# Two layers of segmented attention and feed-forward on one core: other costs in the planner that writes the instruction order, and another table of due times

## The chip, the cores and the metric

The kernel runs on one core of a Trainium2 chip. The metric is the device time of one launch in microseconds. Before the change three runs gave 569.62, 570.12 and 570.35 us, a median of 570.12. Profiled times below come from one more execution, which took 570.93 us; its profile spans 569.2 us from the first to the last instruction.

The engines have short names in the profile: PE multiplies matrices (PEld is its weight load), DVE is the vector engine, ACT the one for activations, POOL is GpSimd, and SP does nothing here but issue transfers.

## The reference

Input `x` has 2048 tokens of 640 numbers. Two rounds of an attention block and a feed-forward block are computed, all with the same weights, each with a residual:

```python
x = x + _A_ref(_layernorm(x, axis=-1), A_wq, A_wk, A_wv, A_wo, A_beta)
x = x + _B_ref(_layernorm(x, axis=-1), B_w1, B_w2)
x = x + _A_ref(_layernorm(x, axis=-1), A_wq, A_wk, A_wv, A_wo, A_beta)
x = x + _B_ref(_layernorm(x, axis=-1), B_w1, B_w2)
```

`_A_ref` has 32 heads of 20 numbers and cuts the tokens into four segments of 512. For each segment it does causal softmax attention inside the segment, and mixes it, by a gate per head, with a read from a memory of the earlier segments:

```python
for s in range(N):
    p = _softmax(logits, axis=-1)
    a_dot = jnp.einsum('bhqk,bhkd->bhqd', p, vs)
    pq = phi(qs)
    num = jnp.einsum('bhld,bhde->bhle', pq, M)
    den = jnp.einsum('bhld,bhd->bhl', pq, z)[..., None] + 1e-06
    o = g * (num / den) + (1.0 - g) * a_dot
    pk = phi(ks)
    M = M + jnp.einsum('bhld,bhle->bhde', pk, vs)
    z = z + jnp.einsum('bhld->bhd', pk)
```

`phi(t)` is t+1 above zero and exp(t) below. `_B_ref` is `relu(x @ w1) @ w2` with 1728 hidden units.

## The kernel before

**Stages.** Eight attention stages follow one another, layer a = 0, 1 by segment s = 0 to 3, and so do eight feed-forward stages. A stage is made of small generators, each of which yields one instruction after another:

- `lnorm` makes the normalised tokens: statistics on DVE (L858 to L860), the inverse deviation on POOL (L865, L867), the scaling on DVE (L871, tile `xn_tok`), and then the transpose to `xnT`, by a crossbar transfer on SP (L847) or by PE (L835). It serves `ln1` ahead of attention and `ln2` ahead of the feed-forward.
- `proj_kq` (L941) and `proj_v` (L988) are the projections. `relay_dma` moves a part of keys and queries through DRAM (writes L1023, reads L1036) because a head has 20 rows, and four heads share 128 partitions.
- `scores` (L1280 on PE, L1291 and L1294 for the exponential on ACT, the causal mask L1270 on POOL), `apply` (L1362: probabilities times values), `turn` (crossbar L1461, division and addition L1396 to L1414 on DVE).
- `mem_write` and `mem_read` are the memory: crossbar L1117 and L1125, `phi` on ACT and DVE (L1133, L1134, L1136; L1193 to L1200), products L1143 and L1230, and L1160 to L1219 on DVE.
- `o_turn` transposes a tile of 128 tokens of the attention's output by crossbar (L1516, tile `oT`, two buffers), `out_proj` multiplies it (L1526), and `add_half` adds the residual on DVE (L1468).
- `ffn` is L1580 (512 columns) with the ReLU on DVE (L1561) or ACT (L1562), the rest of the hidden units (L1592), and L1610 (320 columns).

PE has a mode: scores use it in four groups of rows, `apply` in four groups of columns, L1592 in halves, and all else in full.

**The order.** No loop fixes which instruction comes next. While the program is built, `Sched` in the host's Python plays all generators against a clock of its own, engine by engine, and writes down for each engine the order that comes out, with semaphore waits where an operand comes from elsewhere. On the chip each engine runs its list strictly in order. The rule is:

- `_best` works out for each waiting instruction when it could start: when its operands are ready, its buffers free, and its engine free. An instruction with several engines to choose from (`evac`: DVE or ACT) gets the one that ends it first.
- `run` takes the instruction with the earliest start; among equals the one with the earlier due time. Due times come from `TABLE`, a packed list with one number for each instruction, which `ranked` unpacks. So there are two passes: a first one that only finds the instructions' names, and a second one with the table's due times.
- What an instruction costs the clock is written in constants: `dve_ns`, `act_ns` and `mm_ns` for the engines, and for transfers `issue` on SP, a rate, and a latency. For a crossbar transfer of n blocks (40 for a 128x640 tile, as in L847 and L1516) the plan counts `XB_NS + XB_TILE * n` ns on SP, then some 15 ns per block on the transfer engines, then `XB_LAT`. A transfer issued by SP between 15 and 125 us gets `LOAD_LAT` more, because weights are being loaded then.
- If the plan's PE is idle for long enough, `_filled` puts multiplications of an identity matrix there (L769), which compute nothing that is used.

The constants and the two places that the change touches, as they stand before:

```python
XB_NS, XB_TILE, XB_LAT = 200.0, 27.0, 1700.0
LOAD_FROM, LOAD_TO, LOAD_LAT = 15000.0, 125000.0, 4000.0
...
    r = ready + SEM_NS + (PE_MARGIN if e == "pe" else 0.0)
    start = rank = max(self.free[e], r)
...
def dve(n, mode, fn, waits=(), acq=(), extra=0.0, users=1, early=0.0):
    return Op([("dve", dve_ns(n, mode) + extra, 95.0, one(fn))], waits, acq, users, early=early)
```

The argument `mode` of `dve` is the number of elements that DVE is taken to do in a cycle: 4 for L871, L1134 and L1198, 2 for L1136, L1200 and L1414, and 1 for nearly all else, L1163, L1404 and L1409 among them.

Of the kernel before, what the change touches and what calls it, by code (L numbers as in the profile page):

```python
# [134 lines left out]
class Op:  # L135
# [4 lines left out]
    def __init__(self, alts, waits, acq=(), users=1, mode="full", dma=None, early=0.0, hold=()):  # L140
        self.alts = alts
        self.waits = [t for t in waits if t is not None]
        self.acq = acq
        self.hold = hold
        self.users = users
        self.mode = mode
        self.dma = dma
        self.due = -1.0
        self.early = early
        self.patience = PATIENCE  # L150

# [9 lines left out]
XB_NS, XB_TILE, XB_LAT = 200.0, 27.0, 1700.0  # L161
# [7 lines left out]
LOAD_FROM, LOAD_TO, LOAD_LAT = 15000.0, 125000.0, 4000.0  # L169
# [18 lines left out]
class Sched:  # L188
    def __init__(self, prog, dues=None):
        self.P = prog  # L190
        self.dues = dues
        self.free = {e: 0.0 for e in ENGS}
        self.t = {}
        self.events = {}
        self.fresh = []
        self.active = []
        self.waiting = {}
        self.cur = None
        self.count = 0
        self.ids = set()  # L200
        self.dma_free = 0.0
        self.mode = "full"
        self.log = []
        self.now = -1.0
        self.fill = None
# [71 lines left out]
    def _best(self, op, resv=None):  # L277
# [10 lines left out]
        for k, (e, hold, tail, make) in enumerate(op.alts):  # L288
            r = ready + SEM_NS + (PE_MARGIN if e == "pe" else 0.0)
            start = rank = max(self.free[e], r)  # L290
# [36 lines left out]
    def run(self):  # L327
        while True:
# [45 lines left out]
            if e == "pe":  # L374
                self.mode = op.mode
            if op.dma is not None:
# [29 lines left out]
c-m!JTaX>qb={}?_U(K7zUR*SCC!W^MglzmNyZopA!IP-86XA>31FvUr$~i-  # L406
n4(+`0jE;=%tstk{z?3i4=PTPj{xOVQnno1<%*wFAWA|J4A@vivOpt&n3raD)?VjyPmicuw{Lf!bN1P1pZ!>SpZgJaiPYsTi6xO==}uffD}5P~
*R&%OcuM7CxW-bInhfBsCOy21WKKRRnLL8~7WyC4E70Rkv?gdfu2<piR?r<spBF(jlf!6lqV3nZA8l7l1J5m4(Svxp7T;}XJq0SMT!yDirsaK|
$DKV5qhBmLakriGMfmK+-CoXTboYRsjcrN=&-
?Jb5<F*k8j&q{KM!6iGANg0#4g@<WenHt_{K6SH(>lH@IJwqD?oQQ#`G}DFLgJ5cjJ8rJ@<fCUABUHl{{?0??=!!APaf}*0fbVj`4NO@wz^U_a  # L410
@B-=r2(^+tIR9oV=;K@N{XA$2cg=VE!1Kw&jF=3ZwT>+76@d!mL-Jt%hGGN5R!7XRgS{&uo?3z}fF(O?QCyb+TXX$EvTEYvdM4?Rt#68{bE8|6
6hp@Alx`Zn+8V_WnM(L~h5}+aZUKp~pku{VqKJId=0Xr2ix+-
Y=g4#lvz4d_RcqmoeiV7=2VeCEq{$NpLv>&e~XqNqdKUZ8afpP8Ri9v}TZU1)o$@6Iq8wHNvj+W0P(hb63%)jyW56YNKZYK0A=)F|27A(wW1xh
t?EQPGu5%*nr$mqE{1?2GL^-pDRdX0&QKq@8HR_tBIB$;eHqT4L}ZU&>V;4NAWoT-ffTD=(h#hXTL{r-
GezQkkmHx+=*)kYaRy=BcM0{T7&qVlfR|bk6?x_^n4!Uy5PA3inE{{qkl?GO{nJ$NGYZ5*iM@EOrl4G>uh-5C2wgYQ+T(e6=?e~B-
q9C5au3%R$L;h`T(qK6q+`UUVV96cYyCLxId};<bU<3yr-
u93BJ$k{aD#yd0A&*i!<P>haITVZX@iDlOqcec!~KGagU<nDZfU1>)6t!okYC1H>xq)WA1j$w~j5<VwAOHfvO9m9kn_R^ds7<ze~b+-
_z60M{IEAO3$@Yiz|3`@>TwJNx53AE9ap?4mM_UK@L$dd(3skp)Kzf72h~~^ZBYJ36^<G_@;G{RBdD$_=rmLM)b9QbS3=u!hHG2dRRd|&bS=n+
^>-9g#Ior@##Mq-
k#Qo`?fJ}y(E?Qb)eYS3fJU{^>5ylsPx_yys75vNJ={rZ<2|ZX(LdK3w>DwPfOY;_Gv@^&cX(w(tbz9SkFny`%_xw{N}yi(Uek1*j@|L^w(EmF  # L420
;%Y6Bz-|`?7CLyYrQ__>s+I(1`0VpgZ?Iy;jn(=y#vX6eyTwW%-%Qag`YQ<Wu>(8jXm-+=PQmk*-
Uwq*GcOgmn3WL>uTEE7Qddj(2QJKwM{b3@698}AJW2&JvCbPI|xrS2Jh3rx58MLOCTxsv{vXv6n3X<;|Vpef}M}V&-pXGk%+<-
dRpa5j)1ERTBondZDy7{Rw#iQ{e`XZu>3c!7qrE7)C13Lc+U59vhW8+Nj3L+l^~t`H!AJANw>Ml;^RVRtA%{xLaR6YPA=zW$wzGXmZ?H6^+2tL
_`kjIKbtk)ufbC_%`^@>!Gc}j(^0y$5Bb$N_#t<Z9d*N9TOP;NVyW4h3%1cH_NiU0FD<yK0|{-+YP)xu(Z~EnpS0h@ep#el4EEo^o-
}Arxkryn@<>SCw{G@DuJC-Wh&<jGd0RAlw*L8Z6nw|JHi9mj6?nRFq1UdYleXejb%lRbT8*E@>qaH;S}XZAuY2CR#U-1}C9E2i-
j{vdhDXeMdcE6d@!Yzwx~SN7hii(jUvIu9`>mEVtE`E(@^#qEnl|}1#Y!Xk$GV(>MOYkJ)<LnoGA=&QE@!ET$7@TNuUcsRy1s<IXVth^1J!l(U
e%ar-S1fiUck#-
VXfv#y@o8acMNP20ePves`sp_@9P${pVqg4>Cc0oxbQ&=o);MbI+*1Q5Ka$P^Iy=j|AZwkWAtUfFiniwA^)TwN1vX2pljMA=Lx*<anSx1cwEES
lzK1<4!UR?m!InhaPe_-1K_0wu1@HJCd6Z&yX)n9`VD<ZY&GZAu-
z0gmh0r7^@QGxxu4RrdNtNK2KpvH>$eO&dILNy<823+`2|SfEHK*J;A>cZqyM9ymR~R`ts$<yr>3XB)O+NI`Wu}Cs(cZCYYaRutNFBb$f=H1zp  # L430
Fn0ZaaZ732@yBwVY>&`w$}=t0PZ10ZM1IN(+5oGiquBnEvPFX9_!H+PkJEiBsxh(7OHt`NpbxkDcLpj52!_sL|nlhW<9{EO`2XUJKrAXT~tkh2
T45qS8A0?u75EK^7LH&f)HT9l{z9%1^b%emBa$s?jvRyAND7Ad9=@`?>^5yMb_RMJwQIRlljf2Rf$jHLSY}4HyT-I_RFH?mI?m^LjU9*I&hR7d
ZSy^jHD^r}S-Tr~`!*9Bo7Y3v4-y-R^^eL;iAt>qxn}6|^pE!d!6~JfEjFoX3jK>VJTLTj4ppH{G&`vIrd+gm%4)-
=6?kdrN#?Zz{aRvD1d{tHAuD;Mua533(WrVA8eRvcc?Q8X3hLGm|E;_<e|_mc3kuY$*jI%P_tZGMg^?EUD!=bMX+obPN7C!_IcNzt6c{pl$hh4
-{G$H!Y{#E3k(BXdlP>K5~h^yx^L+cCnj%(9DokjL7kYM!=PueOMW{<vyh!T6{E4idep;9&N=$ZytN?mzOk0%2ilojrrau8RacwsRxuB%a#JM<
lZVO@se|vZSr&*SgBgVE8dI7;xV4d|7!5&GmdtMP+8$KZB(m>WgB#p!iU$%b3R+6h;=@~R6%oDSJdO)Dq>-
t^Ndqc)?*}Khq#mr!~w0Ql4G?zGSmv(-zuV#_3jk$>UeY{P->8Ozot$JgKw6h3!KIUK8RUWXcKAVSzNW?!7)$IrT-UhOF(F8m~DV^*;!yqKcYs
C&1TAUmbFV%6BQbhkIE6&|G}yUik#{>cV%f;|6P41=qVm#blw>vn$7EV&gW_g@s(e(kD>h_izH-2Eh435Vtb$0Jm#(`vc#x_0_vq*am18m-
0X;~l1&IY4fs3XfzhB3aagfQ?$L!<o&?WF<N^6@xf{OvPWiN4CG)V}hvf!2gl{HaU#+3HMXEltn{$wXMT8o6_}B0@Z|Q#WI1L_tgcViE(TZ9{W
s!b2;hf)<*Y!<U#1wY(hlo6f@cv1?j5QIn|7-  # L440
Al3^q6g>ze?_3SayvH2ENFA}#r2{9cDycdFm{Zpiu)W|_m_a1cGJtc(3MXdZ>c52*2Jp0>^X$SA!k<z-
fM3;KL7Za{mQa{0Px@bOST?126x`qt@HGFHYq@?g})+m@tiwrmxot;D01U}<&I&k(J;@+I^g$D7yI_o9z!SPQ*c`0SC4d*<ss+wk;2)WoWX<vZ
)<qYq%VHnIq-JKakU7V}!cY+L2Qv#PW5ntL+ZADwsY=*6W({y{V5lBQLEh~KBR8nmJ&Uk1fTHKCmt509YdS0L9}%5GTpL@lo3TCAzbY-
N&ity9l@EvO4xyRiPd!RI_=c8@lR@2jCcV>|I<y#e%k<iqNQw?tjJ7P~p69;sIuAJdSRT4i<}I@L!8g?R4vvJyL~F?&@oLK*#HW??nPoec83U+
#%c0qYFP5sm5p@;oJFjmiAu60k%A`BqmBI;(;u@+GY^YtN{iNyx&Rlvoe_tS0#Ph|9y6)ugfvFK`@q;287o5oq&kY8Am2ZE9M+h4qhPj>`~(pL
*xn$}RC1q65*nXpg(X-
Me6ZbRyKC%nlDzPXCB+M*FK_tkv=S>h26VX2R?w3i)a(H@SqB$^?A2Ibxdoc{Md{ka56}RfIjX>r;IH827?F#@j#%Ci5qvm^HvQ`fX<fx6h#b5
$BpB!gyLNXS)(T-qCNOkFVJ_Aju}HoMv&~;kZ7f_Z3=nkCyZq$Y4P3p*F2C;*Ak=JVwh|V+3o_>-8x6UGO_6Y2AkI2jwpKn-Tda^h<Syk}w}_U
hoL?at3I`YLiXszv;mc_?y5S!>pTLO7Gdl4mIT`;Cc>rw2L}uh~Kn0LtjHzqu`~1wsmbX78=(66INzZIp#jc_;r}FGavK`eC_OD0`0b+eR|$L_
<0VV@~r+2_hLVNT_3(7f*nt>=dEHHMu(M^gP8X(>B}a#?^EEji*?@%&WF&~By%k}J<qyPk6Jk`dl&wOduZ{z2X9no^i42w1grTx-kL@Y<IPxz3  # L450
l-Y?lia&4M0eYYxHXBW)__mXf+wv~t9&f8SaX}y8GT!L+Ckmx(&kS=-
*007R;Zf$cxE#na)*f5Dp=_t_bUb+JMEYP?z@r*$|}sM?4yR6T~*<iA42~cB10R$^C1$Nk6zT<=(&gJXJcB0=YI;?b{8m(!YW(X-
yvxB9&&HIkI5b6y-#ay;+^-
$kIM(|)xlv8Emf}Pl(XLq^kT8y_^zwaC(dAX!=Ur0ZV+6Xga=rqf85P5)4LJ!p2dnTa~)z_v%j7^FW*8hv+wI!tG-
UY?S8Bt`&!&z)qh*qT>XuU3P4_C@@OY5)tPgAl?6;uu4}*LTtKpUHXfC#;~O>O{)Z~hNx;C-rYh*OE-ETOaZ&M!OVnMc=z5;&QY+PAqk!{z0i8
zjMOO(pC=0cnC7mkj*R6ubj5g*Zx~TqC2`hI2`#t6^XkMXM(`rE6Nm0=~qaIOBGJ09hhYJioT~s}0i)!DDi%K<ZFUeNmu3E}5W&&Dmmw4OY^qE
joj&bMfF!83UTwW7R3;Z_AJZUi4o6%Zkb)%e3*ooX%v0ls9JFG(Fxrmq91!kBPdbu;&W^{ZB*k%@Y3u^JH1~1%a&N~ikw{c%zFpq1vwu-
DbkvYWq1F)j!o#Ch<`G&LH=YTxnrr^i6%gb(5?t}gR0b-_MuvV1f?WA1t?y_1w_6Bxi9NfQ-ym$@syo8K&8#sGKP2LuZ6U67s@tMM`qjGHB{9s
hnS0i{rt1dQqI_P)~nov&Wjou_~>I0o5j5D|4JC8B9yOeLnm^&r%j<aeUu##)>yy|PDu}_|HReJ6*thoc5-
5q6&kfX5YN%T445?b6Sqv<vBR}1s-  # L460
IhR9vTgC2%c>Xm9X|>tEOQbf=yln?^#hqf6nsaJC*pTZ8`mR9o7a;X9YWghpb%qgj5Y}&z$o%G#TCQ8+`E(U`hNh-Dass_<%rsWBit9MWPKW0e
(7O_`csp9QqQ!jpB)HrP9tJVfDyU9k?kVtV5y7|`!mf;?#jx`Q9VPDR5xq=d<Q!J9s1vL{P4ZN-%?v)GhpeO5Hu4kkd~#X0FuJse5PPf-
^umd9AM-EjrSQ`gP_{Kq;yQ&{9nr)HD5RWa6}?t;p5C^Pwb^NQ#90%bZjUnJOaKqBfWK*;L@w$iEN}_WqoBHlr$Z(w;7F`>kn?+a4>Iy+@YcrZ
EcmYx4VdJc;LdAdg*YK$l)9jY@H__({ef1`B%yX~RE9!T=Tfw1(&33<hj_V8k5r?s849XXZ@a-CR@m00h7S<I)p+jMlG8-
fDRsHYQ`SscL`3KG4XqGW**^|EO0N>PrUAG3lh=$`yw1FBmb7Z@mr~;gh!irSDy!LLpx9(fO1^94uSOKo;Cia$A?8d8*Xd6<GR~3)WZIyW_*zA
s@zi63Dq9lfYB4D#lw6B6JYx0lnxTJ-
e%w%Ag%XIlhJ?|mOG)^QKP8PibGLeN>fE4Ia=hFru1Vm(9;zVqP|ay`R4e2>epHjI$bvuakeepGaEJUh_%027+TuM%lQZ9p9JLmDSXAnTtlsaZ
Rcu?~A0~rX%`*MFjsK}0Eig!poMenLRmwh>oIiKV&qjS)CE$U2(1jM`QlIyhZB)XJn%oSxw8JWzVFf*Af0dARbQoV-
# [10 lines left out]
def one(fn):  # L479
    return lambda *s: [(lambda e: fn(e, *s), True)]  # L480
# [10 lines left out]
def dve_ns(n, mode):  # L491
    return 66.0 + n / (0.96 * mode)
# [1212 lines left out]
```

## Time and profile before

| | before |
|---|---|
| median of three runs | 570.12 us (569.62 to 570.35) |
| the profiled execution | 570.93 us, of which the profile spans 569.2 us |
| PE busy | 558.4 us, 98% |
| DVE busy | 425.8 us, 75% |
| ACT busy | 424.5 us, 75% |
| POOL busy | 215.4 us, 38% |
| granted clock of PE | 1.0 in all windows from the start on |

An engine's busy time is the union of its instructions. A matmul's end is modelled and overlaps the next one's start, so a PE that is 98% busy need not run at its peak: what counts is how far apart the starts of its matmuls lie. DVE, ACT and POOL are idle when they wait for an operand, and this costs nothing as long as PE doesn't wait for them. Busy time of a DVE or POOL instruction contains what it stood still in the middle.

The load isn't even. These rows of the windows view have, for each stretch, the busy us of PE, PEld, DVE, ACT and POOL (instructions in brackets), the clock, the share of the transfer engines and the rate:

```profile
40.00:60.00 20.00, 20.00 (x177) 9.19 (x178) 18.18 (x35) 19.14 (x24) 10.05 (x15) 1.00 0.69 148
80.00:100.00 20.00, 19.72 (x205) 10.36 (x204) 19.47 (x48) 18.50 (x23) 13.28 (x21) 1.00 0.82 144
150.00:200.00 50.00, 48.92 (x499) 25.98 (x498) 47.19 (x117) 43.94 (x53) 21.53 (x33) 1.00 0.41 73
500.00:550.00 50.00, 50.00 (x299) 28.38 (x296) 15.21 (x37) 15.31 (x26) 3.01 (x8) 1.00 0.22 48
```

Up to 200 us DVE is busy more than nine tenths of the time, and ACT nearly so. In the last 50 us both are busy three tenths of it, and PE has a long run of feed-forward work alone.

### The profile page before, as it was taken

The page shows a single profiled execution, that of the slowest core. Times are in us where ns is not written, and L with a number is a line of the kernel's source. Part 1 is how long each engine was busy: PE and PEld are TensorE (multiplying, and loading weights), DVE is VectorE, ACT ScalarE, POOL GpSimd, SP SyncE. Part 2 cuts the span into 40 slices and gives each one's busy share as a digit, 9 for nine tenths or more (in the row PEclk, how much of TensorE's full clock was granted, in tenths as well). Part 3 has the DMA queues.
Part 4 walks back from the last instruction along what each step waited for, and adds up shares of the span by engine and source line. Part 5 has one row for each costly group of instructions (what it writes and reads, how often), then busy time and mean ns, then how long its engine had stood idle before and what let it go on. Part 6 is the DMA issues. An engine that isn't in the chain of part 4 may idle for free.

```text
span 569.2 us, 12508 instructions
## 1 busy us (share of the span) xinstructions
PE 558.4 (98%) x5113; PEld 296.0 (52%) x5113; DVE 425.8 (75%) x1020; ACT 424.5 (75%) x519; POOL 215.4 (38%) x343
## 2 busy tenths in 40 slices
PE   8999999999999999999999999999999999999998
PEld 4454445445554445645446554564444654656655
DVE  6689999999999869876689964898767872725202
ACT  4899899998889978778888887977898677332140
POOL 4374447544444434443334423524233422302000
PEclk9999999999999999999999999999999999999999
DMA  6436859766343446454146831386313820432201
GB/s 219 119 89 144 158 123 156 224 150 109 66 91 70 62 71 88 83 97 80 29 77 112 128 43 20 56 122 105 59 21 62 136 69 1 77 81 43 69 0 47
DMA packets 126609, 50.62 MB, mean 89 GB/s; under 512 B 112120, under 2 KB 124600, under 8 KB 126552
## 3 DMA queue, kind: packets, MB, share of 16 engines
q1 hardware_dynamic: 124568, 42.19, 40.7%
q0 software_dynamic: 1552, 7.29, 4.6%
q8 instruction: 40, 0.66, 0.5%
q10 hardware_dynamic: 432, 0.34, 0.2%
q14 instruction: 17, 0.14, 0.1%
HBM read 15.16 MB, written 7.37 MB: 40 GB/s over the span
## 4 chain that ended last, share of the span: by engine, by line
PE 79%; DVE 12%; ACT 4%; DMA 3%; POOL 1%; issue 1%
PE ps L1610 18%; PE ps L1580 17%; PE ps L941 12%; PE ps L1280 7%; PE ps L1526 7%; PE ps L988 7%; PE ps L1362 6%; ACT PT L1294 2%; DMA oT<-o_sb 2%; DVE xn_tok L871 1%; DVE stats L858 1%; DVE x_sb L1468 1%; DVE stats L859 1%; PE ps L1143 1%; PE ps L1230 1%; DVE ktok L1136 1%
## 5 line engine op out<-in xcount | busy, mean ns | idle before, releaser
L1294 ACT ACTIVATE PT<-ps 128x1024 bf16<-128x1024 f32 x256 | 248.3, 1025 | 46.8 <-PE ps L1280 45.9
L1270 POOL TENSOR_SCALAR_AFFINE_SELECT PT<-PT 128x512 bf16<-128x512 bf16 x256 | 171.5, 687 | 262.7 <-ACT PT L1294 218.4
L1610 PE MATMUL ps<-wb,hT 128*128 128x320 bf16 x896 | 136.2, 299 | 1.0 <-DVE x_sb L1468 1.0
L1580 PE MATMUL ps<-xnT,wb 128*128 128x512 bf16 x520 | 126.8, 380 | 0.2 <-DVE hT L1561 0.2
L1468 DVE TENSOR_TENSOR x_sb<-x_sb,ps 128x320 bf16<-128x320 bf16 x128 | 60.7, 479 | 69.9 <-PE ps L1610 47.3
L1610 PEld LDWEIGHTS ps<-wb,hT 128*128 128x128 bf16 x896 | 83.2, 98 | 39.3 <-issue 7.6
L1580 PEld LDWEIGHTS ps<-xnT,wb 128*128 128x128 bf16 x520 | 48.0, 98 | 57.8 <-issue 7.0
L1291 ACT ACTIVATE PT<-ps 128x1024 bf16<-128x1024 f32 x64 | 62.5, 1032 | 14.4 <-PE ps L1280 14.1
L1562 ACT ACTIVATE hT<-ps 128x512 bf16<-128x512 f32 (+1 forms) x62 | 36.1, 583 | 43.6 <-PE ps L1580 42.8
L941 PE MATMUL ps<-xnT,wq_p 128*128 128x512 bf16 x200 | 57.3, 380 | 0.3 <-DVE o_sb L1219 0.3
L988 PE MATMUL ps<-wv_r,xnT 128*128 128x320 bf16 x320 | 57.2, 300 | 0.0
L941 PE MATMUL ps<-xnT,wk_p 128*128 128x512 bf16 x200 | 56.0, 380 | 0.0
L1526 PE MATMUL ps<-wo_r,oT 128*128 128x320 bf16 x280 | 51.8, 299 | 1.2 <-DMA oT<-o_sb 1.1
L1362 PE MATMUL ps<-PT,va 128*32 128x128 bf16 (+3 forms) x896 | 40.8, 302 | 0.0
L988 PEld LDWEIGHTS ps<-wv_r,xnT 128*128 128x128 bf16 x320 | 29.5, 98 | 18.8 <-issue 2.8
L928 DVE CAST kq<-ps 128x512 bf16<-128x512 f32 x45 | 30.8, 685 | 11.1 <-PE ps L941 10.7
L1561 DVE TENSOR_SCALAR hT<-ps 128x512 bf16<-128x512 f32 (+1 forms) x50 | 33.2, 666 | 7.1 <-PE ps L1580 6.9
L871 DVE TENSOR_SCALAR xn_tok<-x_sb,mv,rstd 128x640 bf16<-128x640 bf16 x64 | 33.3, 529 | 4.1 <-POOL rstd L867 2.7
L1280 PE MATMUL ps<-kq 20*128 20x512 bf16 (+3 forms) x560 | 35.3, 301 | 0.2
L1526 PEld LDWEIGHTS ps<-wo_r,oT 128*128 128x128 bf16 x280 | 26.4, 98 | 16.1 <-issue 2.1
L858 DVE BATCH_NORM_STATS2 stats<-x_sb 128x6 f32<-128x320 bf16 x64 | 29.5, 465 | 1.8 <-DMA x_sb<-in_A_x_dram 1.5
L1362 PEld LDWEIGHTS ps<-PT,va 128*32 128x32 bf16 x896 | 18.9, 96 | 22.7 <-issue 10.2
(113 smaller groups left out, 626.6 us busy)
## 6 DMA issues: line engine op xcount, KB each, us to landing
kq_scr<-kq SPq DMA_DIRECT2D x28, 120.0 KB
kqL<-kq_scr SPq DMA_DIRECT2D x28, 120.0 KB
out_dram<-x_sb SPq DMA_DIRECT2D x16, 160.0 KB, 1.8
wb<-in_B_w_dram POOLq DMA_DIRECT2D x5, 432.0 KB, 4.3
x_sb<-in_A_x_dram POOLq DMA_DIRECT2D x3, 640.0 KB, 5.2
wb<-in_B_w_dram POOLq DMA_DIRECT2D x2, 640.0 KB, 5.4
kq_away<-hT SPq DMA_DIRECT2D x5, 256.0 KB, 3.2
kq<-kq_away SPq DMA_DIRECT2D x5, 256.0 KB, 3.4
```

The costliest lines, as they stand in the source:

```text
L871: tn, bx = yield dve(D, 4, lambda e, a, t=t: e.tensor_scalar(a, x_sb[:, t, :], mv[:, t, 0:1], rstd[:, t:t + 1], ALU.subtract, ALU.mult), [ ...
L941: fn = lambda e, bank, k=k, w_p=w_p, c=c: e.matmul(bank, w_p[:, k, c * 128:(c + 1) * 128], xnT[:, k_, :, k, :], start=(k == 0), stop=(k == ...
L988: fn = lambda e, bank, k=k, i=i, hf=hf: e.matmul(bank[:, 0:320], xnT[:, k_, i, k, :], wv_r[:, k, hf * 320:(hf + 1) * 320], start=(k == 0), ...
L1270: tm = yield pool(590.0, lambda e: e.affine_select(out=reg, in_=reg, pattern=[[0, 4], [1, 128]], compare_op=ALU.is_ge, fill=0.0, base=0, c ...
L1280: fns.append((lambda e, x=x, j=j, hh=hh, N=N, o=o: e.matmul(ps[:, hh, o:o + N], kq(b, gg[x], 0)[32 * hh:32 * hh + DH, 128 * j:128 * j + 12 ...
L1291: fn = lambda e: e.activation(PT[:, :, 2 * k:2 * k + 2, 1024:1280], bs.ap.rearrange("p h (x t) -> p x h t", x=2), ACT.Exp, scale=SCALE)
L1294: fn = lambda e: e.activation(PT[:, items[0], 2 * k:2 * k + 2, c0:c0 + 512], bs.ap, ACT.Exp, scale=SCALE)
L1362: return [(lambda e, hh=hh, j=j: e.matmul(bank[32 * hh:32 * hh + 32, 128 * j:L], v_flat[b][:, (j * H + 8 * hh + g) * E1:(j * H + 8 * hh + ...
L1468: ta = yield dve(320, 1, lambda e: e.tensor_tensor(xa, xa, bk.ap[:, 0:320], ALU.add), [tk], early=HOT)
L1526: fn = lambda e, bank, k=k, hf=hf, o=ot.ap: e.matmul(bank[:, 0:320], o[:, k, :], wo_r[:, k, hf * 320:(hf + 1) * 320], start=(k == 0), stop ...
L1580: fn = lambda e, bank, k=k, dc=dc: e.matmul(bank, w1_r[:, k, dc * 128:(dc + 1) * 128], xnT[:, k_, :, k, :], start=(k == 0), stop=(k == FC ...
L1610: fn = lambda e, bank, dc=dc, q=q, h=h, hf=hf: e.matmul(bank[:, 0:320], h, w2_r[:, q, hf * 320:(hf + 1) * 320], start=(dc == 0), stop=(dc ...
```

## The change

All of it lies in the planner; no instruction's operation, shape or operand is rewritten.

1. DVE instructions with `mode` above 1, and the copies of `permute` (L740), are marked `port=True`. In the plan a marked DVE instruction doesn't start before the last POOL instruction planned so far has ended, and a POOL instruction (other than a transfer) doesn't start before the last marked DVE instruction planned so far has ended.
2. `XB_LAT` goes from 1700 to 2300 ns, `LOAD_LAT` from 4000 to 2500 ns, and the rate of the relay's transfers (L1023, L1036) from 85 to 80 bytes per ns.
3. `TABLE` holds other numbers.

```diff
-    def __init__(self, alts, waits, acq=(), users=1, mode="full", dma=None, early=0.0, hold=()):
+    def __init__(self, alts, waits, acq=(), users=1, mode="full", dma=None, early=0.0, hold=(), port=False):
...
+        self.port = port
...
-XB_NS, XB_TILE, XB_LAT = 200.0, 27.0, 1700.0
+XB_NS, XB_TILE, XB_LAT = 200.0, 27.0, 2300.0
...
-LOAD_FROM, LOAD_TO, LOAD_LAT = 15000.0, 125000.0, 4000.0
+LOAD_FROM, LOAD_TO, LOAD_LAT = 15000.0, 125000.0, 2500.0
...
+        self.port = {"dve": 0.0, "pool": 0.0}
...
+            if e == "dve" and op.port:
+                r = max(r, self.port["pool"])
+            if e == "pool" and op.dma is None and hold:
+                r = max(r, self.port["dve"])
...
+            if e == "dve" and op.port or e == "pool" and op.dma is None and hold:
+                self.port[e] = end
...
-    return Op([("dve", dve_ns(n, mode) + extra, 95.0, one(fn))], waits, acq, users, early=early)
+    return Op([("dve", dve_ns(n, mode) + extra, 95.0, one(fn))], waits, acq, users, early=early, port=mode > 1)
...
-                                           lambda e, o=o, i=i: e.activation(o, i, ACT.Copy)))], w)
+                                           lambda e, o=o, i=i: e.activation(o, i, ACT.Copy)))], w, port=True)
...
-                        tk, sc = yield dma("sp", scw_sem[z][r], 122880, lambda e, s_, f=f: f(e), ev, [SCR[z]], rate=85.0)
+                        tk, sc = yield dma("sp", scw_sem[z][r], 122880, lambda e, s_, f=f: f(e), ev, [SCR[z]], rate=80.0)
```

The other three `rate=85.0` of `relay_dma` change in the same way. Built, the changed program has a different order on every engine. PE has the same matmuls, but for 26 identity multiplications in place of 21. All instructions of `evac`, `permute` and the ones in `consts` that may go to either of two engines are shared out nearly as before: 222 on DVE (218 before), 141 on ACT (143), 3 on POOL (5).

## The prediction, made before the changed kernel ran

> **What bounds the kernel now.** First the head of the page.
>
> ```profile
> span 569.2 us, 12508 instructions
> PE 558.4 (98%) x5113; PEld 296.0 (52%) x5113; DVE 425.8 (75%) x1020; ACT 424.5 (75%) x519; POOL 215.4 (38%) x343
> ```
>
> PE sets the end. But matmul ends are modelled, so the question is how much of the 569.2 is PE at its peak. The chain of waits shows undisturbed PE at its end:
>
> ```profile
> 536.32 14.03 PE ps L1580 x65
> ...
> 551.02 15.33 PE ps L1610 x112
> ```
>
> That is 216 ns for 512 columns and 137 ns (starts lie 136 apart) for 320. From the starts of matmuls in the timeline, a change of PE's mode adds 95 ns (231 instead of 136 after a 320-column matmul). I laid PE's order end to end with these: 0.216, 0.136, 0.109, 0.056 and 0.039 us for 512, 320, 256, 128 and 84 columns, a quarter of it each for scores and apply, and 95 ns for each of 400 mode changes. The sum is **547.1 us**. The real last matmul starts 19.1 us later than in that sum. Start by start: 1.2 us before the first matmul; 3.4 us in the opening (slow first matmuls, first norm); some 6 us spread evenly (0.15 us in each 12.5 us, also where nothing waits); and about **8.5 us in some twenty places between 25 and 450 us where PE stands still**. The rest, 569.2 - 547.1 - 19.1 = 3.0 us, is the last matmul, residual and store. The sum for the new order, with as many matmuls (five more identity ones, 0.3 us inside the opening's wait) and 399 mode changes, is 547.2. So no PE work is won: **the change can only win from those 8.5 us, or add to them.**
>
> What stops PE there? The chain, window by window:
>
> ```profile
> 66.71 1.42 DVE xn_tok L871 x2
> 68.13 0.61 DVE kq L928
> 68.74 0.05 issue
> 68.79 0.25 PE ps L1230 x2
> ```
>
> PE lost 0.57 us here. It waited for L928, which stood behind two L871 that took 1.42 us. The timeline has POOL and DVE in the same place:
>
> ```profile
> 66.66 1.30 POOL L1270 TENSOR_SCALAR_AFFINE_SELECT PT<-PT 128x512 bf16<-128x512 bf16 x2
> 66.71 1.42 DVE L871 TENSOR_SCALAR xn_tok<-x_sb,mv,rstd 128x640 bf16<-128x640 bf16 x2
> ```
>
> and the answers for the two lines say what one takes, min/median/max in ns:
>
> ```profile
> L871 DVE TENSOR_SCALAR xn_tok<-x_sb,mv,rstd x64: 349/444/865, 6.8 to 527.3; 128x640 bf16<-128x640 bf16 x64
> L1270 POOL TENSOR_SCALAR_AFFINE_SELECT PT<-PT x256: 624/634/1824, 21.7 to 491.8; 128x512 bf16<-128x512 bf16 x128
> ```
>
> Two masks and two L871 that started together needed about twice the DVE time. The same pair stands before other stalls:
>
> ```profile
> 80.11 1.67 POOL L1270 TENSOR_SCALAR_AFFINE_SELECT PT<-PT 128x512 bf16<-128x512 bf16 x2 [0.92 <-ACT PT L1294]
> 80.16 1.12 DVE L1136 TENSOR_TENSOR ktok<-ktok,etmp 128x1024 bf16<-128x1024 bf16 x1
> ...
> 163.39 1.98 POOL L1270 TENSOR_SCALAR_AFFINE_SELECT PT<-PT 128x512 bf16<-128x512 bf16 x3
> 163.46 1.41 DVE L871 TENSOR_SCALAR xn_tok<-x_sb,mv,rstd 128x640 bf16<-128x640 bf16 x2
> ```
>
> PE then lost 0.43 us at 81.1 and 0.52 at 164.7. Three more stalls have a stretched packed operation ahead in the chain: 0.77 at 155.5 (L1414, 0.75 against a median of 0.32), 0.37 at 178.8 (L1200), 0.78 around 403 (L871, 0.86; ahead of it a 4.51 us crossbar). Together **3.44 us behind DVE**.
>
> The second kind is SP's queue:
>
> ```profile
> 436.42 3.74 SPq L1023 DMA_DIRECT2D kq_scr<-kq  x4
> 440.20 3.44 SPq L1516 DMA_TRANSPOSE oT<-o_sb  x1
> ...
> 390.81 0.58 PE L1526 MATMUL ps<-wo_r,oT 128*128 128x320 bf16 x3 [1.10 <-DMA oT<-o_sb]
> ```
>
> L1516 lands 2.7 us after its issue in the median, but 5.6 us behind four relay writes; PE waited 0.22 us for that one at 445.5, and 1.26 at 389.4 for a transpose that stood behind two others on SP: **1.48 us**. The remaining 3.6 us follow ACT (0.55 at 27.1, 0.34 at 35.2, 0.5 near 107) or a burst of DVE work that isn't packed (0.85 near 372).
>
> **The change part by part.**
>
> *Port marking.* It removes no wait on the chip: whoever meets the other still stands still. It changes what the plan believes, so PE work lands where operands are really ready. Against each line's tenth percentile, marked DVE instructions lose 6.3 (L871), 4.6 (L1414), 2.4 (L1136), 1.3 (L1200) and 2.3 us (L1198), POOL 14.5 (L1270): the old plan has none of this. DVE is busy over nine tenths until 200 us, so there the plan runs ahead of the chip. If the new plan covers all of it, 3.44 us go; if the chip's pairs meet elsewhere, none.
>
> Here a rule speaks against the change. In the Trainium skill, "SBUF — State Buffer", section "SBUF: two separate sides", the port pair shared by DVE and GpSimd is an exclusive lock that whoever *starts* first holds for the whole instruction; DVE takes it in two-port modes, and also, against a GpSimd operation that reads SBUF, with two SBUF inputs. The trace agrees with the lock (1.42 us for two L871 of 0.35 to 0.44 beside two masks). The change marks `mode` above 1, so it leaves out 48 instructions with two SBUF inputs: L1163, L1404, L1409. By their rows they lose 2.0, 1.5 and 1.7 us, 5.2 of the 22.1 us that both sorts lose, a quarter. And "first" is the plan's first, not the chip's. By the marking alone the gain is 3.44; by the rule three quarters of it, 2.6, less where order flips. I take **2.3**.
>
> *Crossbar latency 1.7 to 2.3 us.* With issue (1.28) and blocks (0.6), the plan allowed a 40-block transpose 3.58 us; now 4.18. Of 80 such transposes in the trace 15 took longer than 3.58 and 11 longer than 4.18, so it helps few; in general it buys distance. In PE's new order there are 16 to 22 us of PE work between a stage's last apply and its first out-projection in stages 2, 4 and 6 (22.0, 21.1, 18.7), where the old has 14.8, 14.0, 12.5. Stage 6, which waited at 445.5, has its first two L1516 behind four relay reads, its third behind two stores and transposes; between tile 1's end and tile 3's start lie 5.65, 7.15 and 12.2 us of work in stages 5 to 7, enough for the worst 5.6. Between 0 and 1.48, I take **1.0**.
>
> *Load latency 4.0 to 2.5 and rate 85 to 80.* In the load window a 40-block transpose is now allowed 6.68 us instead of 7.58; there the trace has 2.7 to 4.8. Plain transfers there took 2.0 to 5.4. Cover stays: 0. The slower rate lengthens a relay transfer by 0.09 us in the plan only: 0. POOL's loads stay in their order behind the same masks.
>
> *New order and table.* What becomes tight is told by laying PE's order end to end. From a feed-forward's last matmul to the next layer's first L988 the old order has 15.9, 11.0, 10.8, 12.7 us of PE work; the new 17.4, **10.0**, 15.7, **9.8**. The trace's chain (residual, statistics, L867, L871, transpose landed) took 10.3, 9.5, 7.8, 9.1. So both tight places just hold; either could lose up to 0.5. From stage 1's out-projection to its L1580 the old has 14.8, the new 13.9, and the chain took 14.2: **0.3 lost**. Other chains are longer than needed. DVE and ACT share the evacuations as before, so no engine takes over. The opening: the first L871 now comes after the statistics of all four tiles, some 0.75 us later, but the third and fourth then wait less for POOL and PE (0.65 and 0.53 us before); -0.4 to +0.7, I take 0.
>
> **Sum.** 569.2 - 2.3 - 1.0 + 0.3 = 566.2 us of span. The profiled execution took 1.7 us more than its span, and 0.8 more than the median: 570.93 - 3.0 = 567.9 there, **567.1** for a median of runs.
>
> **Rivals.** About 0.2% (1.1 us) can be told from no change.
>
> A, forecast: less than 569.0, most likely 567.1. At best all 4.9 us and half of the other 3.6 go: 563.4. Chance 0.58.
>
> B, no change: the same number of surprises in new places, because the plan is still not the chip (DVE's unpacked instructions, ACT, relay traffic). For it: the new order differs from the first rows on, and 3.6 of 8.5 us have causes that the change doesn't model. Against: the causes it models made the larger part. 570.1. Chance 0.15.
>
> C, slower: the two tight turns of the layer. A chain of 12.5 us costs 2.5 + 2.7 there, giving 567.1 + 5.2 = 572.3; at 14.2, what the stage 1 chain took, 575.7. It decides from 11.4 us on (2 x 11.4 - 19.8 = 3.0). For it: the chain ends in L871 and a transpose, the two things that stretch. Against: the plan puts no matmul ahead of operands that it believes late, and it now believes the transpose 1.5 us later than the median. Chance 0.27, with other new stalls of that size.
>
> The range 563.0 to 573.0 leaves out the tail of C and the best of A; the forecast's own range is 563.4 to 569.
>
> **What would show it.** Right: the shift against the end-to-end sum grows by less than 10 us between 12 and 475 us (14.4 before); L1270 and L871 shrink towards 634 and 444 ns in the mean (687 and 529 now); no stall behind L871 or L1516 above half a microsecond. Wrong: L988 of stages 5 and 7 waiting for `xnT`, or as many stalls as before with L871, L1136 or L1414 ahead of them in the chain.

## The result, and the profile after

Four runs of the changed kernel gave 565.08 to 565.58 us, a median of **565.47 us**, against 569.87 us (569.18 to 570.35) of four runs before: a ratio of 0.9922, 95% interval 0.9905 to 0.9940. Between the medians lie 4.4 us. The profiled execution spans 563.8 us, 5.4 less than before; 1.0 of that is because the profiled execution of before was slower than its median by so much more than this one is.

The head of the page after:

```profile
span 563.8 us, 12521 instructions
PE 556.4 (99%) x5115; PEld 297.7 (53%) x5118; DVE 420.9 (75%) x1024; ACT 422.5 (75%) x517; POOL 214.9 (38%) x341
```

No engine has less work worth speaking of. What changed is who the end waits for. The shares of the chain that ended last, before:

```profile
PE 79%; DVE 12%; ACT 4%; DMA 3%; POOL 1%; issue 1%
```

and after:

```profile
PE 91%; DVE 5%; ACT 2%; DMA 1%; issue 0%; SPq 0%
```

In the prediction's end-to-end sum of PE's own work (547.1 us before, 547.2 after) the last matmul came 19.1 us late before and comes 13.6 us late now. By the same sum, places where PE stands still cost 8.6 us from 25 us on before and 4.2 now; from 175 us on it is 3.65 before and 0.41 now. The six largest of PE's waits by line, before (line and engine waited for, us in total, times, longest):

```profile
PE ps L835 <- DVE xn_tok L871: 1.5, 2, 0.8
PE ps L810 <- DVE ktok L807: 1.2, 1, 1.2
PE ps L1526 <- DMA oT<-o_sb: 1.1, 1, 1.1
PE ps L1610 <- DVE x_sb L1468: 1.0, 2, 0.5
PE ps L1280 <- ACT PT L1291: 0.7, 2, 0.5
PE ps L1230 <- DVE kq L928: 0.4, 1, 0.4
...
```

And all that the same view lists after (every line number is ten higher there):

```profile
PE ps L820 <- DVE ktok L817: 1.2, 1, 1.2
PE ps L1290 <- ACT PT L1304: 1.2, 2, 0.8
PE ps L998 <- DMA wv_r<-in_A_wv_dram: 0.8, 1, 0.8
PE ps L1240 <- DVE o_sb L1229: 0.4, 1, 0.4
PE ps L845 <- ACT xnT L853: 0.2, 1, 0.2
PE ps L1096 <- issue: 0.2, 1, 0.2
```

The 1.2 us for `ktok` and most of the waits for `xn_tok`, `xnT` and `wv_r` belong to the opening. The waits for the residual `x_sb`, for `oT` and for `kq` are gone. At the place that the prediction opened with, the masks and the scaling no longer run side by side:

```profile
65.77 1.22 POOL L1280 TENSOR_SCALAR_AFFINE_SELECT PT<-PT 128x512 bf16<-128x512 bf16 x2
...
66.89 0.49 DVE L1229 TENSOR_TENSOR o_sb<-ps,rmem 128x320 bf16<-128x320 f32 x1
67.30 0.44 DVE L881 TENSOR_SCALAR xn_tok<-x_sb,mv,rstd 128x640 bf16<-128x640 bf16 x1
67.65 0.68 DVE L938 CAST kq<-ps 128x512 bf16<-128x512 f32 x1
```

The two masks end at 66.99, L881 starts after them and takes 0.44 us, its undisturbed time; beside the masks DVE does work that isn't packed (packed operations are those with a `mode` above 1). Meetings haven't gone everywhere, as these two groups show (busy us, mean ns, idle before). Before:

```profile
L1270 POOL TENSOR_SCALAR_AFFINE_SELECT PT<-PT 128x512 bf16<-128x512 bf16 x256 | 171.5, 687 | 262.7 <-ACT PT L1294 218.4 <-ACT PT L1291 44.1
...
L871 DVE TENSOR_SCALAR xn_tok<-x_sb,mv,rstd 128x640 bf16<-128x640 bf16 x64 | 33.3, 529 | 4.1 <-POOL rstd L867 2.7 <-DMA xnT<-xn_tok 0.5 <-PE ps L835 0.5
```

After:

```profile
L1280 POOL TENSOR_SCALAR_AFFINE_SELECT PT<-PT 128x512 bf16<-128x512 bf16 x256 | 173.1, 692 | 235.8 <-ACT PT L1304 195.5
...
L881 DVE TENSOR_SCALAR xn_tok<-x_sb,mv,rstd 128x640 bf16<-128x640 bf16 x64 | 30.0, 482 | 3.2 <-POOL rstd L877 3.1
```

The mean of L881 fell from 529 to 482 ns, and that of the mask rose from 687 to 692. The largest loss left outside the opening is a stretch in which DVE is busy without a break with operations that aren't packed, from the chain of waits:

```profile
157.12 0.49 DVE stats L868
157.62 0.39 DVE stats L869
158.01 0.39 DVE x_sb L1478
158.40 0.12 DVE mv L870
158.51 0.55 DVE oraw L1400
159.07 0.16 DVE rmem L1225 x2
```

PE stands still for some 2 us between 154 and 161 us; its last wait there, for L1229 at the end of the burst, is what holds up the work that follows. The marks say nothing about such a burst.

### The profile page after: what moved, and what is told of

Same layout as the page of the kernel before. It is cut to its first block, busy times and chain, and to the rows that moved or that the text cites. A ratio compares the mean times of both kernels' runs of the same rounds, so it can differ in the third digit from the quotient of the medians.

```text
span 563.8 us, 12521 instructions
## 1 busy us (share of the span) xinstructions
PE 556.4 (99%) x5115; PEld 297.7 (53%) x5118; DVE 420.9 (75%) x1024; ACT 422.5 (75%) x517; POOL 214.9 (38%) x341
## 4 chain that ended last, share of the span: by engine, by line
PE 91%; DVE 5%; ACT 2%; DMA 1%; issue 0%; SPq 0%
PE ps L1590 21%; PE ps L1620 20%; PE ps L951 15%; PE ps L1290 9%; PE ps L998 8%; PE ps L1536 7%; PE ps L1372 7%; DMA wv_r<-in_A_wv_dram 1%; PE ps L1153 1%; PE ps L1240 1%; ACT PT L1304 1%; DVE x_sb L1478 1%; PE ps L1602 1%; DVE stats L868 1%; DVE stats L869 1%; PE ps L1096 1%
## 5 line engine op out<-in xcount | busy, mean ns | idle before, releaser
L1620 PE MATMUL ps<-wb,hT 128*128 128x320 bf16 x896 | 133.0, 300 | 0.1
L1590 PE MATMUL ps<-xnT,wb 128*128 128x512 bf16 x520 | 127.4, 380 | 0.0
L1572 ACT ACTIVATE hT<-ps 128x512 bf16<-128x512 f32 (+1 forms) x65 | 37.4, 577 | 54.5 <-PE ps L1590 53.9
L1590 PEld LDWEIGHTS ps<-xnT,wb 128*128 128x128 bf16 x520 | 47.2, 98 | 54.8 <-issue 7.6
L998 PE MATMUL ps<-wv_r,xnT 128*128 128x320 bf16 x320 | 57.0, 300 | 0.9 <-DMA wv_r<-in_A_wv_dram 0.8
L951 PE MATMUL ps<-xnT,wq_p 128*128 128x512 bf16 x200 | 55.8, 380 | 0.1
L1536 PE MATMUL ps<-wo_r,oT 128*128 128x320 bf16 x280 | 50.2, 300 | 0.0
L1571 DVE TENSOR_SCALAR hT<-ps 128x512 bf16<-128x512 f32 (+1 forms) x47 | 31.9, 680 | 12.9 <-PE ps L1590 12.6
L998 PEld LDWEIGHTS ps<-wv_r,xnT 128*128 128x128 bf16 x320 | 29.6, 98 | 20.8 <-issue 2.6
L938 DVE CAST kq<-ps 128x512 bf16<-128x512 f32 x43 | 29.4, 683 | 10.0 <-PE ps L951 9.6
L1536 PEld LDWEIGHTS ps<-wo_r,oT 128*128 128x128 bf16 x280 | 26.8, 98 | 15.5 <-issue 2.0
L881 DVE TENSOR_SCALAR xn_tok<-x_sb,mv,rstd 128x640 bf16<-128x640 bf16 x64 | 30.0, 482 | 3.2 <-POOL rstd L877 3.1
```

Source lines behind the costliest of these rows:

```text
L951: fn = lambda e, bank, k=k, w_p=w_p, c=c: e.matmul(bank, w_p[:, k, c * 128:(c + 1) * 128], xnT[:, k_, :, k, :], start=(k == 0), stop=(k == ...
L998: fn = lambda e, bank, k=k, i=i, hf=hf: e.matmul(bank[:, 0:320], xnT[:, k_, i, k, :], wv_r[:, k, hf * 320:(hf + 1) * 320], start=(k == 0), ...
L1536: fn = lambda e, bank, k=k, hf=hf, o=ot.ap: e.matmul(bank[:, 0:320], o[:, k, :], wo_r[:, k, hf * 320:(hf + 1) * 320], start=(k == 0), stop ...
L1572: lambda e: e.activation(d, bk.ap[:, 0:n], ACT.Relu), [tk] + hs[0].old + (hs[1].old if dc >= NSTG // L else []))
L1590: fn = lambda e, bank, k=k, dc=dc: e.matmul(bank, w1_r[:, k, dc * 128:(dc + 1) * 128], xnT[:, k_, :, k, :], start=(k == 0), stop=(k == FC ...
L1620: fn = lambda e, bank, dc=dc, q=q, h=h, hf=hf: e.matmul(bank[:, 0:320], h, w2_r[:, q, hf * 320:(hf + 1) * 320], start=(dc == 0), stop=(dc ...
```

## The experiments

Two theories were held against each other at first. **Port**: the chip loses time because packed DVE operations and masks meet, and the plan now avoids meetings that matter. **Luck of the order**: any other table gives another order, and this one is better for reasons of its own. Later a third came up: that the planner's new latencies do the work.

For each kernel one more figure helps, which is the planner's and not measured: the moment at which its own clock has PE's last instruction ended. The **gap** is the profiled span less that figure. It contains the tail after the last matmul, which is about 3 us in both kernels. "Clock lost" is the span times one minus the mean granted clock. Span, gap and clock lost are of the profiled execution alone; the medians are of 4 to 10 executions, and each ratio is to executions of the kernel before made beside them (medians of 569.64 to 570.31).

| kernel | costs | table | median us | ratio to before | span | plan's end | gap | clock lost |
|---|---|---|---|---|---|---|---|---|
| before | old | old | 569.87 | 1 | 569.2 | 557.3 | 11.9 | 0 |
| after | new | new | 565.47 | 0.9922 (0.9905 to 0.9940) | 563.8 | 559.0 | 4.8 | 0 |
| e1, short masks | old | old | 565.27 | 0.9919 (0.9898 to 0.9939) | 563.4 | 557.3 | 6.1 | 0.3 |
| e2, short masks | new | new | 566.37 | 0.9930 (0.9906 to 0.9953) | 564.5 | 559.0 | 5.5 | 1.7 |
| e3 | new | old | 582.51 | 1.0222 (1.0204 to 1.0240) | 580.8 | 576.7 | 4.1 | 1.7 |
| e4 | old | new | 576.05 | 1.0107 (1.0088 to 1.0127) | 574.7 | 564.8 | 9.9 | 1.7 |
| e5 | new, crossbar 2200 | new | 569.90 | 0.9988 (0.9970 to 1.0005) | 568.1 | 561.8 | 6.3 | 0 |
| e6 | old, crossbar 1800 | old | 572.91 | 1.0043 (1.0026 to 1.0059) | 570.4 | 561.8 | 8.6 | 0.4 |
| e7 | port, old latencies | new | 570.28 | 0.9994 (0.9980 to 1.0007) | 568.5 | 563.2 | 5.3 | 1.7 |
| e8 | new latencies, no port | new | 581.78 | 1.0181 (1.0142 to 1.0220) | 581.4 | 569.8 | 11.6 | 3.4 |
| e9, short masks | as e4 | new | 570.81 | 1.0016 (1.0003 to 1.0029) | 567.9 | 564.8 | 3.1 | 0 |
| e10, short masks | as e8 | new | 575.58 | 1.0113 (1.0097 to 1.0129) | 573.7 | 569.8 | 3.9 | 1.7 |
| e11 | new, two-input marked | searched | 568.11 | 0.9973 (0.9963 to 0.9982) | 566.7 | 561.8 | 4.9 | 0 |

With the median, less the 1.7 us that lie outside the span, in place of the profiled span, the gaps are 10.8 (before), 9.5 (e4), 9.4 (e6) and 10.2 (e8) without marks and 4.8 (after), 4.1 (e3), 6.4 (e5), 5.3 (e7) and 4.6 (e11) with them. The two kinds lie apart either way. The 0.3 and 0.4 us of clock lost in e1 and e6 fall behind the last matmul and cost nothing.

### The meetings taken away, the order kept (e1, e2)

The mask works on one of its 128 columns instead of all, so POOL is done in a third of the time and rarely meets anyone; these kernels leave out the causal mask inside the diagonal blocks. Neither order changes, since the plan still counts the full mask.

```diff
-                        out=reg, in_=reg, pattern=[[0, 4], [1, 128]], compare_op=ALU.is_ge, fill=0.0, base=0,
+                        out=reg[:, :, 127:128], in_=reg[:, :, 127:128], pattern=[[0, 4], [1, 1]], compare_op=ALU.is_ge, fill=0.0, base=127,
```

In the kernel before:

> The order of before, instruction for instruction, but each causal mask on POOL writes one column instead of 128, so POOL hardly holds the port; this leaves out the causal mask inside the diagonal blocks. Theory P (packed VectorE operations that meet a mask make PE late): the 3.4 us of stalls behind L871, L1136, L1414 and L1200 go, and L871's mean falls from 529 to about 400 ns: 566 to 567 us. Rival L (the stalls are a lottery of order, the meeting with POOL is a bystander): 569 to 570 us.

In the kernel after:

> The order of after with the same one-column masks; the causal mask inside the diagonal blocks is left out. Theory P: the new order already has room for the meetings, so at most 0.8 us is left to win: 564.7 to 565.5 us. Rival L or a third case (the meetings still cost as much as before, and the gain came from elsewhere): 562 to 563 us.

The old order with short masks ran in 565.27 us (564.87 to 565.59), a little less than expected: **as fast as the changed kernel, in an order that was not changed at all**. The timeline of e1 where the prediction had two L871 of 1.42 us together:

```profile
65.98 0.80 DVE L871 TENSOR_SCALAR xn_tok<-x_sb,mv,rstd 128x640 bf16<-128x640 bf16 x2
65.99 0.50 POOL L1270 TENSOR_SCALAR_AFFINE_SELECT PT<-PT 128x4 bf16<-128x4 bf16 x2
66.93 0.69 DVE L928 CAST kq<-ps 128x512 bf16<-128x512 f32 x1
```

And its answers for the two lines (min/median/max in ns):

```profile
L871 DVE TENSOR_SCALAR xn_tok<-x_sb,mv,rstd x64: 350/442/489, 6.9 to 521.5; 128x640 bf16<-128x640 bf16 x64
...
L1270 POOL TENSOR_SCALAR_AFFINE_SELECT PT<-PT x256: 197/207/1398, 21.9 to 485.5; 128x4 bf16<-128x4 bf16 x128
```

The longest L871 is 489 ns where it was 865. By mean, L1198 falls from 447 to 362 ns, L1414 from 404 to 319, L1136 from 728 to 677, while what is neither packed nor fed by two SBUF operands stays (L928 685 and 688, L1468 479 and 483). Every stall that the prediction put behind a packed operation is gone (68.0, 81.1, 155.5, 164.7, 178.8, around 403), and so is the one near 372 that it had put down to unpacked work: there, from 368.5 us on, two L871 of 0.75 and 0.67 us stand beside two masks that start at 368.4, and delay what follows. PE's stalls go from 12.0 to 6.4 us, the opening's 3.4 among both. What stays is the waits for ACT and the one for `oT`:

```profile
PE ps L1526 <- DMA oT<-o_sb: 0.9, 1, 0.9
...
PE ps L1280 <- ACT PT L1291: 0.7, 2, 0.5
PE ps L1280 <- ACT PT L1294: 0.3, 1, 0.3
```

In the new order the same edit won next to nothing: 566.37 us, more than either theory expected. Three of its four executions have a clock episode of 1.7 us (last section); the one without took 564.34 us, 1.1 below the median of the changed kernel. So meetings cost 4.4 us in the old order and about 1 in the new one. Short masks also make the probabilities ready 0.4 us sooner. If that were the gain of e1, e2 should show it too; and PE's weight loads ahead of L1362 waited 3.6 us for masks before and still 3.2 in e1.

### Costs and tables crossed (e3, e4)

e3 is the kernel after with the old `TABLE`, e4 the kernel before with the new one; nothing else differs.

> The new costs (port, latencies, rate) with the table of before. Theory P (the costs do it, the table only breaks ties): 565.5 to 567.5 us. Rival T (the table does it): 569 us or more.

> The costs of before with the new table. Theory P: 568.5 to 571 us. Rival T: 565 to 567 us. If both mixed kernels are slower than both originals, a table belongs to its costs, and neither part alone explains the gain.

Both are slower than either kernel, the third case named beforehand: 582.51 and 576.05 us. But the plans already end at 576.7 and 564.8 us, so each table fits only the costs that it was made with, and a table says nothing alone. What the two runs do tell is the gap. The plan with port marks is followed within 4.1 us, the one without by 9.9.

### One constant moved (e5, e6)

```diff
-XB_NS, XB_TILE, XB_LAT = 200.0, 27.0, 2300.0
+XB_NS, XB_TILE, XB_LAT = 200.0, 27.0, 2200.0
```

The same in the kernel before, from 1700.0 to 1800.0. Each moves a table slightly off its own costs.

> After with a crossbar latency of 2200 in place of 2300 ns, nothing else; its own plan ends PE at 561.8 us. Theory F (time = the plan's own end of PE + what the costs leave out; the first four kernels show 9.9 and 11.9 us from that end to the end of the span with the old costs, 4.1 and 4.8 with the new): span 566.3 to 567.0, time 567.7 to 569. Rival L (any reorder is a lottery): anywhere from 565 to 580, with no relation to the plan's end.

> Before with a crossbar latency of 1800 in place of 1700 ns; its own plan also ends PE at 561.8 us, as that of the run with 2200. Theory F: 10 to 12 us more than that, span 572 to 574, time 573 to 575.5, although the plan is as long as that of the run with 2200. Rival L: no relation.

The plans grow to 561.8 us both times, and the runs to 569.90 and 572.91. So 100 ns of a latency cost 2.6 us in the kernel before (570.31 beside it) and, by the ratios, 3.8 in the kernel after. In e5 the latency is the shorter one, so what grew there is the plan's misfit to its table; in e6 the two aren't separated. 4.4 us won between two kernels means little until this is told apart. The gaps, 6.3 with marks and 8.6 without, again differ, though less than expected (4.5 to 5.2, and 10 to 12).

### Port and latencies separated (e7, e8)

e7 is the kernel after with `XB_LAT` 1700, `LOAD_LAT` 4000 and the rates of 85. e8 keeps the latencies and leaves the exclusion out:

```diff
-            if e == "dve" and op.port:
-                r = max(r, self.port["pool"])
-            if e == "pool" and op.dma is None and hold:
-                r = max(r, self.port["dve"])
```

> The new table and the port marking, but the old latencies and rate; its plan ends PE at 563.2 us. If the marking is what brings the plan near the chip: span 5 to 6 us more, time 570 to 571.5. If the latencies are: 9 us or more, time 573.5 or more.

> The new table, latencies and rate, but no port marking; its plan ends PE at 569.8 us. If the marking is what brings the plan near the chip: span 9 us or more above that, time 580 or more. If the latencies are: 5 us, time 576 to 577.

With the port alone the gap is 5.3 us, or 3.6 without the clock's 1.7; with the latencies alone it is 11.6, or 8.2. That is the kernel after's gap on one side, and on the other e4's, which has neither (8.2 without the clock's part). So **the gap goes with the marks and not with the latencies**: the five plans with marks have gaps of 4.1 to 6.3 us, the four without 8.6 to 11.9. A gap that is small by luck of the order would have had to come out so five times. PE's waits in e8 show what an unmarked plan runs into in this order too:

```profile
PE ps L1286 <- ACT PT L1300: 2.8, 3, 1.8
PE ps L1236 <- DVE o_sb L1225: 2.0, 2, 1.6
PE ps L1236 <- DVE phq L1206: 1.8, 1, 1.8
```

e7 is no slower than before, and no faster. Its plan is 4.2 us longer than that of the kernel after. A table of its own might shorten it; none was made, so what the marks alone would win is not shown. It has no wait above 0.25 us ahead of an out-projection although it plans the crossbar at 1700; e6, with 1800 and the old order, still has one of 0.75 us at 392. The runs therefore don't show that the longer latency is what removed the waits for `oT`.

### Short masks in the unmarked orders (e9, e10)

The mask of e1 in e4 and in e8, orders kept.

> The order of the run with the old costs and the new table, unchanged, with one-column masks; the causal mask inside the diagonal blocks is left out. Its plan ends PE at 564.8 us and the span with full masks was 9.9 us longer. Theory F (unmarked plans lose some 10 us on the chip, of which 5 are meetings of VectorE and GpSimd): span 4 to 6 us above the plan's end, 569 to 571, time 570.5 to 572.5. Rival (the gap is something else): span 573.5 or more, time 575 or more.

> The order of the run with new table and latencies but no marking, unchanged, with one-column masks; the causal mask inside the diagonal blocks is left out. Its plan ends PE at 569.8 us and the span with full masks was 11.6 us longer. Theory F: span 4 to 6.5 us above the plan's end, 574 to 576.5, time 575.5 to 578. Rival: span 580 or more.

e9 takes 5.2 us less than e4, e10 6.2 us less than e8, and the gaps come down to 3.1 and 3.9 (4.2 and 4.1 by the medians). In the pair e9 and e4 this isn't the clock: most executions of both lost the 1.7 us, and those that lost nothing took 569.14 to 569.68 us in e9 and 575.35 in e4. In the pair e10 and e8 some 1.7 of the 6.2 us is the clock. In PE's waits of e4 and e9 one sees which ones go. e4:

```profile
PE ps L1231 <- DVE o_sb L1220: 1.5, 1, 1.5
...
PE ps L1527 <- DVE x_sb L1469: 1.0, 1, 1.0
PE ps L1144 <- DVE ktok L1137: 0.8, 2, 0.6
...
PE ps L1231 <- DVE phq L1201: 0.5, 1, 0.5
```

e9:

```profile
PE ps L1231 <- DVE o_sb L1220: 1.4, 1, 1.4
...
PE ps L1527 <- DVE x_sb L1469: 0.2, 1, 0.2
```

`ktok` and `phq`, both written by packed operations, drop out of the list, and the wait for the residual falls from 1.0 to 0.2. The wait of 1.4 for `o_sb`, which is unpacked, stays, and so do 2.4 us for the exponential on ACT.

### The operations that the marks leave out (e11)

The prediction held that L1163, L1404 and L1409 (here ten lines higher), with two operands in SBUF, should be marked as well. e11 marks them, with a table adapted to it by a short search that started from the new one:

```diff
+def dve(n, mode, fn, waits=(), acq=(), extra=0.0, users=1, early=0.0, two=False):
+    return Op([("dve", dve_ns(n, mode) + extra, 95.0, one(fn))], waits, acq, users, early=early, port=mode > 1 or two)
...
-                        maskg[:, 4 * h:4 * h + 4].rearrange("p g r e -> p (g r e)"), ALU.mult), [tu] + mg, [BDS[h]])
+                        maskg[:, 4 * h:4 * h + 4].rearrange("p g r e -> p (g r e)"), ALU.mult), [tu] + mg, [BDS[h]], two=True)
```

> After, with L1163, L1404 and L1409 (two operands in SBUF, mode 1) marked as well, and a table adapted to that by a short search; its plan ends PE at 561.8 us, 2.8 later than after's. If these 48 operations are what is left of the gap between plan and chip: span 3 to 4 us above the plan's end, 565 to 566, time 566.5 to 567.5. If they matter little: 4.5 to 6.5 us, time 568 to 570. It beats after in neither case.

568.11 us, 2.6 more than the kernel after. Its plan is 2.8 us longer and its gap the same, 4.9 against 4.8. These operations do stretch: by mean L1163 takes 667 ns before and 496 with short masks, L1404 606 and 485, L1409 877 and 819. But keeping them away from the masks brings the chip no nearer to the plan. With a better table this could look different; that wasn't tried. No kernel here that keeps the whole mask beats the changed one.

## Why the prediction was right, and where its sizes were off

It gave 567.1 us, faster, with 563.0 to 573.0 as its range. The direction, the mechanism and the range held. The sum took 3.0 us off; 4.4 came off between the medians. That it came so near is in part luck: a longer plan (1.7 us) and new stalls (1.4 us) had no term in it, and a port term that was too small made up for them.

- **No PE work is won; the change can only win standstills.** Right: the end-to-end sum moved by 0.1 us, and the lateness of the last matmul fell from 19.1 to 13.6 us.
- **Port marking, 2.3: the term that was mis-sized.** The prediction saw 3.44 us behind packed operations, took three quarters of it for the two-input operations left unmarked, and less for flipped order. Without any meeting the same order runs about 4.4 us faster (e1), which is more than the 3.44, since the stall of 0.85 near 372 was a meeting's too; and neither deduction was due. The plan with marks kept its gap at 4.8 although two-input operations still meet masks (L1409's mean is 877 ns in both kernels), and e11 shows that marking them closes nothing more. That such operations lose time beside masks is right (L1163 667 ns, and 496 with short masks); what failed is the step from "these operations lose time" to "PE loses a quarter of the gain". A stretched operation costs only where PE waits for what it holds up.
- **The plan itself got longer**, which the prediction had no term for. The marks and latencies move the plan's end from 557.3 to 559.0. So the whole gain is the chip keeping up: the gap fell by 7.1 us between the profiled executions (6.0 by the medians), of which 1.7 was paid for in advance.
- **Crossbar latency, 1.0.** The waits for `oT`, 1.48 us, did go. The smallest slack of a transpose before its out-projection is 0.4 us now, where it was 0.0 to 0.1 in stages 5 and 6, and 5 of 80 transposes took longer than 4.18 us instead of 11. Whether the constant did this stays open: e7 has the old constant and none of these waits either.
- **Load latency and rate, 0.** Nothing in the trace speaks against it, and e7 and e8 show no gain from them.
- **Tight chains, +0.3, and rival C.** Not paid. `xnT` of stage 5 landed 2.3 us ahead of its L998, that of stage 7 2.0 us; in stage 1 `xnT` for the feed-forward landed 0.1 us before L1590, and PE didn't stand still. Of the three, only that last place was as tight as said.
- **Opening, 0.** It came out 0.24 us better.
- **What was to show it.** Right: the lateness grew by 9.0 us between 25 and 474 us (14.2 before); no stall above 0.5 us behind L881 or L1536's transpose. Wrong: the mask did not shrink towards 634 ns (687 to 692), and L881 only went half way to 444 (482). Meetings went only in part, and those that are left cost PE little (about 1 us, e2): the plan now leaves room for them.

Two remarks of the prediction don't hold. DVE is over nine tenths busy only from 40 us on; between 20 and 40 us it is 8.4 to 8.7 of every 10. And the best of A, 563.4, lies inside its range of 563.0 to 573.0.

Put together, 3.44, 0.85 and 1.48 us of stalls went, 5.8 in all, from 8.6. Of the 4.2 us that PE stands still now after 25 us, 1.4 are new: the burst at 154 to 161 alone costs 2.0, at a place that cost 0.8 before.

## What to carry to other kernels

A plan made on the host should count what operations of two engines cost each other, not only how long each takes alone: here the plan with exclusion ends later on paper and sooner on the chip. Whether it has to know which pairs exclude each other isn't shown: no run gave the plan simply longer costs for the same operations. Judge a planner by the gap between its end and the chip's, apart from how short its plan is, because a table searched under one set of costs is worth nothing under another. To price a contention, take the contender away and keep the order.

## What the runs showed of the hardware

A short stall can cost more than itself, through PE's granted clock. In e2 PE was busy for 1.81 of 3.0 us, and in the next 3.5 us the clock was 0.51 (windows view: PE, PEld, DVE, ACT, POOL busy, clock, share and rate of the transfers):

```profile
157.00:160.00 3.00, 1.81 (x41) 0.99 (x36) 3.00 (x12) 2.91 (x4) 1.61 (x4) 1.00 0.09 18
160.00:163.50 3.50, 3.43 (x16) 1.63 (x13) 3.47 (x13) 2.75 (x3) 0.37 (x2) 0.51 0.60 113
```

The kernel after has the same order and kept its clock:

```profile
157.00:160.00 3.00, 2.18 (x43) 0.96 (x40) 2.96 (x12) 2.43 (x3) 1.94 (x4) 1.00 0.03 8
160.00:163.50 3.50, 3.06 (x25) 1.89 (x26) 3.47 (x13) 3.50 (x5) 2.32 (x4) 1.00 0.63 118
```

At the low clock the starts of 320-column matmuls lie 267 ns apart instead of 136, and the episode costs 1.7 us (3.41 us at half the clock). e3, e4, e7 and e10 lost 1.7 us as well, and e8 twice that.

How long PE stands still doesn't decide it alone. The 2.18 us of the kernel after are no more work than the 1.81 of e2: the same stalls come half a microsecond later there, and from 157.5 to 160.5 us its PE was busy for 1.81 of 3.0 us too, at a clock of 1.00 then and after. In e5 PE was busy for 1.40 of the 3.41 us from 96.05 on, and the clock stayed at 1.00. And executions of one kernel differ: of e2's four, one kept its clock (564.34 us, the others 566.19 to 566.57), of e4's four one, of e9's eight three. What decides stays open. For a comparison of kernels it means that 1.7 us may come and go without any change.
